# A gated linear attention feeding a cosine-gated MLP: scores as 48x128 products, value sums and state products in 64-channel pieces, independence by parts

## The chip, the cores and the metric

The kernel runs on one core of a Trainium2 chip. The metric is the device time in microseconds (us) of one execution; lower is better. TensorE (PE) does matrix products into PSUM, VectorE (DVE) and ScalarE (ACT) work on PSUM and SBUF, GpSimd (POOL) on SBUF alone, and SyncE (SP) issues most DMAs. A TensorE product has two instructions: a load of the stationary operand (PEld in the profile) and a matmul that streams the moving operand through it. The array can be divided: a product with a stationary operand of at most 64 rows or columns can be given a part of it, and products on different parts can run at the same time. A "tile size" below is that division: 128x128 is the whole array, 64x64 a quarter, 128x32 a column strip.

## The reference, cut to what matters

```python
def _attn_ref(q, k, v, f_logit):            # (B, H, S, D) = (4, 8, 768, 48)
    f = 1.0 / (1.0 + np.exp(-f_logit))
    state = np.zeros((B, H, D, D))
    for t in range(S):
        state = f[:, :, t, :, None] * state + np.einsum('bhd,bhe->bhde', k[:, :, t], v[:, :, t])
        y[:, :, t] = np.einsum('bhd,bhde->bhe', q[:, :, t], state)
    return y

def _moe_ref(x, w_in, w_out):               # x: (3072, 384), d_ff = 2048
    h = x @ w_in
    g = h * np.cos(h)
    return g @ w_out
```

The attention output, 8 heads of 48 channels side by side (384 channels), is x of the second part. All inputs and the output are float32.

## The kernel before, in words

The recurrence is computed in chunks of 128 tokens, two chunks (g = 0, 1) at a time. Such a pair, n = 0 to 11, is 256 tokens of one batch; three pairs make a batch. Within a pair: gates and their running sums (ex, ln, cum, eb, ei), q and k scaled by them (qm, km), q and k turned so that channels lie on partitions, scores, masked scores, value sums, state products, and the state update. The names below are the steps of the code; `n` is the pair, and a second number the half of the heads (u) or the chunk.

- **tq/tk, qkt.** Pairs 0 to 6 are turned on TensorE (`tr`, L436, against an identity, 8 transposes for a half of the heads) and copied out of PSUM by DVE or ACT. Pairs 7 to 11 (`TURN_QK`) are turned by a DMA transpose on SP's queue instead; these the code calls `turned`.
- **sc, am.** `scores` (L456) multiplies k by q for four heads, 16 products of 48 rows by 64 columns, whose places in the array are r (rows 0 or 64) and x (columns 0 or 64). DVE masks them on the way to SBUF (am, L460).
- **ps, st, sz.** `outer` (L478) forms k times v; DVE adds the old state (st, L496) and scales by the decay (sz, L502).
- **y, yi.** `inner` (y) multiplies values by masked scores, `inter` (yi) the old state by q, both into the same PSUM sum of 384 channels by 256 tokens. Both go through `summed` (L530), which cuts the 384 channels into 12 blocks of 32 columns and orders the products so that four neighbours lie on four different column strips. A head of 48 channels touches two blocks, and its zero-padded values (tile vt) fill the rest.
- **xe.** DVE or ACT copies each chunk's sum to x (L199, the line of a shared copy helper).

The second part runs over units of 128 or 256 tokens (unit m of 2 to 12 is pair m - 1): h (L578) is x times w_in, co (L583) the cosine on ACT, g (L560) the product on DVE, o (L594) g times w_out, ot the copy and out the store. Step h11.21 is unit 11, quarter 2, half 1.

The order of all steps on all engines, with the engine and the PSUM bank or SBUF slot of each, is a list written out by a planner and fixed in the string `ORDER`. Its letters are T for PE, S for ACT, V for DVE, G for POOL, Y for SP. It interleaves the attention of later pairs with the products of earlier units. PSUM is four tiles of two banks each. Two steps on different engines that touch the same PSUM tile would be made to wait for each other; `apart` (L644) declares such a pair independent when their banks differ and they share no SBUF slot.

Step `zf` is a product of zeros that fills TensorE's idle time in the first part of the kernel.

Of the kernel before, what the change touches and what calls it, by code (L numbers as in the profile page):

```python
# [10 lines left out]
BF16 = mybir.dt.bfloat16  # L11
# [4 lines left out]
B, H, S, D = 4, 8, 768, 48  # L16
C = 128
PAIRS = B * S // (2 * C)
PPB = S // (2 * C)
DM, DF = 384, 2048  # L20
# [170 lines left out]
def describe(nc, cpool, ppool, q, k, v, f_logit, moe_w_in, moe_w_out, out):  # L191
# [3 lines left out]
    def tl(shape, dt, name):  # L195
        return cpool.tile(shape, dt, name=name)

    def copy(e, o, i):
        (nc.scalar.copy if e == "ACT" else eng(e).tensor_copy)(out=o, in_=i)  # L199
# [6 lines left out]
    ident = tl([128, 128], BF16, "ident")  # L206
# [4 lines left out]
    if nc is not None:  # L211
# [5 lines left out]
        for r in range(2):  # L217
            s = slice(64 * r, 64 * r + 64)
# [94 lines left out]
    def pair(n):  # L313
        b, c = divmod(n, PPB)
# [49 lines left out]
        if not cut:  # L364
            G.step(f"ad{n}", ("POOL",), lambda e: eng(e).tensor_add(  # L365
                out=sp.ap[:, 0, :, 0:D], in0=soft.ap[:, :, 0, :], in1=soft.ap[:, :, 1, :]), reads=[soft], writes=[sp])
# [23 lines left out]
        for nm, dst, dh, sc, w in (("eb", bt, bth, -1.0, HB + 4), ("ei", bi, bih, 1.0, HB)):  # L390
            if cut:
                for u in us:
                    G.step(f"{nm}{n}.{u}", ("ACT",), lambda e, u=u, dh=dh, sc=sc, w=w: nc.scalar.activation(
                        out=dh[u].ap, in_=pcs[u].ap[:, 0:w], func=AF.Exp, scale=sc),
                        reads=[pcs[u]], writes=[dh[u]], table="E")
            else:
                G.step(f"{nm}{n}", ("ACT",), lambda e, dst=dst, sc=sc, w=w: nc.scalar.activation(
                    out=dst.ap, in_=pcs[0].ap[:, 0:2 * (HB + 4)].rearrange("p (u n) -> p u n", u=2)[:, :, 0:w],
# [5 lines left out]
        for u in us:  # L404
            for j, (nm, src, dec) in enumerate((("qm", qh[u], bth[u]), ("km", kh[u], bih[u]))):
                G.step(f"{nm}{n}.{u}", ("POOL", "DVE") if cut else ("POOL",), lambda e, u=u, j=j, src=src, dec=dec: eng(e).tensor_mul(  # L406
                    out=qkp[u][j].ap[:, :, :, 0:D], in0=swap(src.ap),
                    in1=dec.ap[:, 0:HB].rearrange("p (h d) -> p h d", d=D)[:, None].broadcast_to([128, 2, 4, D])),
                    reads=[src, dec], writes=[qkp[u][j]])
        vb, vt = Val(vbS), Val(vtS)  # L410
# [8 lines left out]

        qkt = [Val(qktS), Val(qktS)]  # L420
        turned = n in TURN_QK
        qkv = lambda u: qkt[u].ap.rearrange("p (j e a g n) -> p j a g e n", j=2, a=2, g=2, e=2)
        for u in us:
            if turned:
                G.step(f"tq{n}.{u}", ("SP",), lambda e, u=u: nc.sync.dma_start_transpose(
                    out=qkt[u].ap.rearrange("p (b n) -> p b n", n=C),
                    in_=qk.ap[:, u].rearrange("p j e h d -> p (j e h d)")),
                    reads=[qkp[u][0], qkp[u][1]], writes=[qkt[u]])
                continue
            pt = Val(p1)  # L430

            def tr(e, u, j, pt):
                o = pt.ap.bitcast(BF16).rearrange("p (j e a n) -> p j e a n", j=2, e=2, a=2)
                for x in range(2):
                    for a in range(2):
                        nc.tensor.transpose(out=o[:, j, x, a, :], identity=ident,  # L436
                                            in_=qkp[u][j].ap[:, x, 2 * a:2 * a + 2, :].rearrange("p h d -> p (h d)"))
            for j in range(2):
                G.step(f"t{'qk'[j]}{n}.{u}", ("PE",), lambda e, u=u, j=j, pt=pt: tr(e, u, j, pt),
                       reads=[qkp[u][j]], writes=[pt], sums=True)  # L440
            G.step(f"qkt{n}.{u}", ("DVE", "ACT"), lambda e, u=u, pt=pt: copy(e, qkt[u].ap, pt.ap.bitcast(BF16)),
                   reads=[pt], writes=[qkt[u]])


        am = [Val(amS), Val(amS)]
        for u in us:
            sc = Val(p2)

            def scores(e, u=u, sc=sc):
                o = sc.ap.rearrange("p (r b n) -> p r b n", r=2, n=C)  # L450
                for a in range(2):
                    for g in range(2):
                        for r in range(2):
                            for x in range(2):
                                s, t = slice(64 * r, 64 * r + D), slice(64 * x, 64 * x + 64)
                                nc.tensor.matmul(o[t, r, 2 * a + g, :].rearrange("p (e n) -> p e n", e=2),  # L456
                                                 lhsT=qkv(u)[s, 1, a, g, x, :], rhs=qkv(u)[s, 0, a, g, :, :],
                                                 start=(a == 0 and g == 0), stop=(a == 1 and g == 1))
            G.step(f"sc{n}.{u}", ("PE",), scores, reads=[qkt[u]], writes=[sc])
            G.step(f"am{n}.{u}", ("DVE",), lambda e, u=u, sc=sc: nc.vector.tensor_mul(  # L460
                out=am[u].ap.rearrange("p r b n -> p (r b) n"), in0=sc.ap.rearrange("p (y m) -> p y m", m=C),
                in1=pmask.rearrange("p a n -> p (a n)")[:, None, :].broadcast_to([128, 8, C])),
                reads=[sc], writes=[am[u]])
# [3 lines left out]
        ps = [Val(p1), Val(p1)]  # L467
# [17 lines left out]
        before = [state.get(b), None]  # L485
        for g in gs:
            view = lambda g=g: ps[g].ap[:, 0:HB].rearrange("p (a n) -> p a n", n=D)
            new, S0 = Val(szS), before[g]
# [24 lines left out]
        py = [Val(p1), Val(p1)]  # L513


        def blocks(h):
            i, j = divmod(h, 2)
            return ((3 * i, 16), (3 * i + 1, 48)) if j == 0 else ((3 * i + 1, 0), (3 * i + 2, 32))

        def summed(work, ops):  # L520
            lanes, left = [[w for w in work if w[1] % 4 == c] for c in range(4)], {}
            for w in work:
                left[w[0], w[1] % 4] = left.get((w[0], w[1] % 4), 0) + 1
            begun = set()
            for k in range(max(map(len, lanes))):
                for w in (lane[k] for lane in lanes if k < len(lane)):
                    g, b = w[0], w[1]
                    c, m = b % 4, b // 4
                    left[g, c] -= 1
                    nc.tensor.matmul(py[g].ap[32 * c:32 * c + 32, C * m:C * m + C],  # L530
                                     start=(py[g].first and (g, c) not in begun),
                                     stop=(py[g].final and left[g, c] == 0), **ops(*w))
                    begun.add((g, c))

        def inner(e):
            summed([(g, b, h, at) for g in range(2) for h in range(H) for b, at in blocks(h)],
                   lambda g, b, h, at: dict(lhsT=vt.ap[:, H * g + h, at:at + 32],
                                            rhs=am[h // 4].ap[:, h % 2, h % 4 // 2 * 2 + g, :]))

        def inter(e):  # L540
            summed([(g, b) for g in range(2) if before[g] is not None for b in range(DM // 32)],
                   lambda g, b: dict(
                       lhsT=before[g].ap[:, b // 3].rearrange("p r d -> p (r d)")[:, b % 3 * 32:b % 3 * 32 + 32],
                       rhs=qkv(b // 6)[:, 0, b // 3 % 2, g, :, :]))
        G.step(f"y{n}", ("PE",), inner, reads=[am[0], am[1], vt], writes=py, sums=True)
        G.step(f"yi{n}", ("PE",), inter, reads=[*qkt, *(s for s in before if s is not None)],
               writes=py if before[0] is not None else [py[1]], sums=True)


        x = Val(xS)  # L550
# [56 lines left out]
    for n in range(PAIRS):  # L607
        pair(n)
    t0 = 0
# [9 lines left out]
def emit(tc, G, tiles):  # L619
    nc = tc.nc  # L620
    plan = []
    for word in ORDER.split():
        name, how = word.split(":")
        plan.append((G.steps[name], LETTER[how[0]], [int(x) for x in how[1:].split(",") if x]))
    assert len(plan) == len(G.steps)
    table, users = None, [[] for _ in tiles]
    for s, e, places in plan:
        for w in s.writes:
            v = w.whole
            if v.pool is not None and v.slot is None:  # L630
                v.slot = places.pop(0)
            w.first, w.final = not w.begun, w.left == 1
            w.begun, w.left = True, w.left - 1
        if s.table is not None:
            if s.table == "E" and table != "E":
                nc.scalar.preload_act_table_set("natural_log_exp_and_others")
            table = s.table
        n0 = nc.next_id()
        s.fn(e)
        made = (nc.find_inst_by_name(f"I-{i}") for i in range(n0 + 1, nc.next_id()))  # L640
        apart(tc, users, s, e, [i for i in made if i is not None])


def apart(tc, users, s, e, made):  # L644


    vals = [v.whole for v in s.reads + s.writes]
    banks = {b for v in vals if isinstance(v.pool, Banks) for b in range(v.slot, v.slot + v.pool.size)}
    places = {(v.pool.name, v.slot) for v in vals if v.pool is not None and not isinstance(v.pool, Banks)}
    for t in {b // 2 for b in banks}:  # L650
        for engine, others, theirs, there in users[t]:
            if engine != e and not banks & theirs and not places & there:
                for b in others:
                    for a in made:
                        tc.declare_no_dep(a, b, reason="the steps use different PSUM banks")
        users[t].append((e, made, banks, places))
        del users[t][:-WITHIN]


# [48 lines left out]
```

## Time and profile before

| | us |
|---|---|
| median of 3 runs (lowest to highest) | 189.03 (188.83 to 189.44) |
| the profiled execution | 188.89 |
| its span, first to last instruction | 186.9 |
| PE busy, 2580 matmuls recorded | 177.5 |
| DVE, ACT, POOL busy | 140.1, 136.2, 102.8 |
| L578 and L594 (h and o), busy | 66.4 and 67.4 |
| L530 (y and yi), L456 (sc), busy over the span | 11.12 and 8.81 |

Busy times are unions of the instructions' spans, so overlapping matmuls count once. The span is what the trace covers; some 2.0 us of the execution lie around it. TensorE's granted clock is 1.00 in the whole span.

### The profile page before, as it was taken

Reading aid. Unit: us, or ns where it says so; the run is one execution under the profiler, and the core shown is the slowest. Engines: PE = TensorE matmul, PEld = TensorE weight load, DVE = VectorE, ACT = ScalarE, POOL = GpSimd, SP = SyncE. Lnnn points to the kernel's source line nnn. Section 1 sums busy time; section 2 is a strip of 40 time slices with the busy share of each in tenths; the row PEclk is TensorE's granted clock in tenths of the full one; section 3 lists DMA queues with packets and bytes.
Section 4 is the critical chain, followed back from the end, with each engine's and each line's share of the span. In section 5 each row is a group of like instructions: output and inputs, shape, how many; then the busy total and the mean of one; then the engine's idle time right before and its main releaser. Section 6 shows DMA issues by size and latency. Waiting matters only on the chain.

```text
span 186.9 us, 6052 instructions
## 1 busy us (share of the span) xinstructions
PE 177.5 (95%) x2580; PEld 127.8 (68%) x2584; DVE 140.1 (75%) x209; ACT 136.2 (73%) x196; POOL 102.8 (55%) x131
## 2 busy tenths in 40 slices
PE   7999779999999999999999899999999999999992
PEld 2455437986668976688866787667777888755661
DVE  4458986994897998999997889978999798530010
ACT  3898596795998999798899797897746887500051
POOL 3058249995586998999947999399910000000000
PEclk9999999999999999999999999999999999999999
DMA  6999999639999981996699599977860000000054
GB/s 152 261 261 298 335 355 339 202 102 301 279 265 281 281 189 48 266 282 173 142 259 237 130 230 194 192 194 65 153 186 4 0 4 0 0 0 4 0 212 166
DMA packets 68058, 32.89 MB, mean 176 GB/s; under 512 B 61120, under 2 KB 66496, under 8 KB 68032
## 3 DMA queue, kind: packets, MB, share of 16 engines
q1 hardware_dynamic: 62512, 30.35, 67.5%
q10 hardware_dynamic: 5520, 2.16, 4.9%
q8 instruction: 20, 0.33, 0.8%
q14 instruction: 6, 0.05, 0.1%
HBM read 25.17 MB, written 4.72 MB: 160 GB/s over the span
## 4 chain that ended last, share of the span: by engine, by line
PE 74%; DMA 10%; DVE 6%; POOL 4%; ACT 3%; issue 1%; ACTq 0%; POOLq 0%; DVEq 0%
PE ps L578 32%; PE ps L594 32%; DMA k<-in_k_dram 8%; PE ps L456 3%; PE ps L530 3%; DMA f<-in_f_logit_dram 2%; PE ps L436 2%; DVE sz L502 2%; DVE ps L496 2%; POOL qk L406 2%; PE ps L478 1%; DVE am L460 1%; DVE x L199 1%; POOL k L353 1%; ACT sp L335 1%
## 5 line engine op out<-in xcount | busy, mean ns | idle before, releaser
L594 PE MATMUL ps<-w_out_bf,g 128*128 128x384 bf16 x384 | 67.4, 326 | 0.0
L578 PE MATMUL ps<-x,w_in_bf 128*128 128x256 bf16 (+1 forms) x624 | 66.4, 264 | 1.0 <-DVE sz L502 0.5
L560 DVE TENSOR_TENSOR g<-ps,co 128x1024 bf16<-128x1024 f32 x48 | 61.2, 1312 | 7.0 <-ACT co L583 6.7
L583 ACT ACTIVATE co<-ps,halfpi 128x1024 bf16<-128x1024 f32 x48 | 52.6, 1114 | 14.0 <-PE ps L578 11.5
L578 PEld LDWEIGHTS <-w_in_bf 128*128 128x128 bf16 x624 | 56.6, 98 | 8.8 <-DVE sz L502 1.0
L594 PEld LDWEIGHTS <-g 128*128 128x128 bf16 x384 | 35.9, 98 | 22.0
L460 DVE TENSOR_TENSOR am<-ps,pmask 128x1024 bf16<-128x1024 f32 x24 | 28.7, 1219 | 4.6 <-PE ps L456 4.2
L406 POOL TENSOR_TENSOR qk<-k,bi 128x384 bf16<-128x384 f32 x22 | 21.8, 1004 | 0.6
L199 ACT COPY ot<-ps 128x384 f32<-128x384 f32 (+1 forms) x16 | 6.9, 461 | 20.0 <-DVE ot L199 15.4
L353 POOL TENSOR_TENSOR k<-k,f 128x384 f32<-128x384 f32 (+1 forms) x12 | 11.2, 936 | 16.4 <-DMA k<-in_k_dram 9.4
L406 POOL TENSOR_TENSOR qk<-q,b 128x384 bf16<-128x384 f32 x20 | 19.8, 1004 | 0.6
L199 DVE COPY ot<-ps 128x384 f32<-128x384 f32 (+1 forms) x10 | 5.0, 511 | 18.2 <-PE ps L594 15.3
L266 PE MATMUL ps<-zero 128*128 128x512 bf16 x58 | 17.0, 427 | 1.5 <-DVE zero L205 1.2
L199 POOL COPY vt<-vb 64x384 bf16<-64x384 bf16 x29 | 14.6, 503 | 2.2 <-ACT vb L199 0.8
L502 DVE TENSOR_TENSOR sz<-ps,b 64x192 bf16<-64x192 f32 x40 | 13.9, 354 | 1.3 <-PE ps L478 0.3
L365 POOL TENSOR_TENSOR sp<-ls 128x384 bf16<-128x384 f32 x10 | 10.0, 1000 | 8.0 <-ACT ls L335 7.9
L496 DVE TENSOR_TENSOR ps<-ps,sz 64x192 f32<-64x192 f32 x32 | 11.7, 366 | 2.3 <-PE ps L530 0.9
L436 PE MATMUL ps<-ident,qk 128*128 128x128 bf16 x112 | 9.9, 219 | 2.4 <-POOL qk L406 1.3
L331 ACT ACTIVATE f<-f 128x768 f32<-128x768 f32 (+1 forms) x14 | 10.4, 749 | 1.9 <-DMA f<-in_f_logit_dram 1.7
L199 DVE COPY qkt<-ps 128x1024 bf16<-128x1024 bf16 x12 | 8.1, 683 | 4.5 <-PE ps L436 4.4
L436 PEld LDWEIGHTS <-qk 128*128 128x128 bf16 x112 | 7.5, 98 | 5.2 <-DVE qk L406 1.6
L266 PEld LDWEIGHTS <-zero 128*128 128x128 bf16 x62 | 5.7, 105 | 7.3 <-issue 2.2
(62 smaller groups left out, 176.3 us busy)
## 6 DMA issues: line engine op xcount, KB each, us to landing
v<-in_v_dram SPq DMA_DIRECT2D x12, 384.0 KB, 6.7
out_dram<-ot SPq DMA_DIRECT2D x22, 192.0 KB, 2.2
f<-in_f_logit_dram SPq DMA_DIRECT2D x9, 384.0 KB, 4.3
q<-in_q_dram SPq DMA_DIRECT2D x9, 384.0 KB, 5.9
k<-in_k_dram SPq DMA_DIRECT2D x9, 384.0 KB, 5.4
g<-in_moe_w_in_dram SPq DMA_DIRECT2D x4, 768.0 KB, 10.7
g<-in_moe_w_out_dram SPq DMA_DIRECT2D x4, 768.0 KB, 7.6
q<-in_q_dram SPq DMA_DIRECT2D x3, 192.0 KB, 5.3
```

Of the source, the lines that this page charges most:

```text
L199: (nc.scalar.copy if e == "ACT" else eng(e).tensor_copy)(out=o, in_=i)
L266: G.step(f"zf{i}", ("PE",), lambda e, dump=dump: nc.tensor.matmul(dump.ap, lhsT=zero[:, 0:128], rhs=zero, start=True, stop=True), writes=[ ...
L353: eng(e).tensor_mul(out=w.ap[:, :, 0, :], in0=w.ap[:, :, 0, :], in1=t.ap[:, :, 0, :])
L406: G.step(f"{nm}{n}.{u}", ("POOL", "DVE") if cut else ("POOL",), lambda e, u=u, j=j, src=src, dec=dec: eng(e).tensor_mul(out=qkp[u][j].ap[: ...
L436: nc.tensor.transpose(out=o[:, j, x, a, :], identity=ident, in_=qkp[u][j].ap[:, x, 2 * a:2 * a + 2, :].rearrange("p h d -> p (h d)"))
L460: G.step(f"am{n}.{u}", ("DVE",), lambda e, u=u, sc=sc: nc.vector.tensor_mul(out=am[u].ap.rearrange("p r b n -> p (r b) n"), in0=sc.ap.rear ...
L496: nc.vector.tensor_add(out=view()[s], in0=view()[s], in1=S0.ap[s, :, r, :])
L502: eng(e).tensor_mul(out=new.ap[s, :, r, :].rearrange("p (u a) n -> p u a n", u=2), in0=view()[s].rearrange("p (u a) n -> p u a n", u=2), i ...
L560: nc.vector.tensor_mul(out=o.rearrange("p b (n e) -> p b e n", e=2), in0=ph.ap.rearrange("p (b e n) -> p b e n", e=2, n=64), in1=co.ap.rea ...
L578: nc.tensor.matmul(ph.ap[:, i * T:(i + 1) * T].rearrange("p (g t) -> p g t", t=C), lhsT=w_in_bf[:, kk, f0:f0 + 128], rhs=xa[:, :, kk, :], ...
L583: G.step(f"co{m}.{j}", ("ACT",), lambda e, ph=ph, co=co: nc.scalar.activation(out=co.ap, in_=ph.ap, func=AF.Sin, bias=halfpi), reads=[ph], ...
L594: nc.tensor.matmul(po.ap[:, 0:DM], lhsT=gT.ap[:, j, i * C:(i + 1) * C], rhs=w_out_bf[:, j, :], start=(po.first and j == 4 * s), stop=(po.f ...
```

## The change

Three edits. `ORDER` stays as it is.

1. **Scores.** For the pairs that TensorE turns (0 to 6), the layout of the turned q and k becomes `(j a g e n)`: the two token halves e of a chunk lie side by side, so that a head's k of a chunk is 128 contiguous columns. `scores` then makes 8 products of 48 rows by 128 columns for four heads instead of 16 of 48 by 64. The transposes write their 128 columns in two strides of 64. Pairs 7 to 11 keep the layout and the 16 products.
2. **Pieces.** `pieces` cuts a range of channels into pieces of 64 where one starts on a multiple of 64 and fits, and of 32 elsewhere. Heads 0, 3, 4 and 7 become one piece of 64 each, heads 1, 2, 5 and 6 two of 32. In `inter`, each two heads (96 channels) become one of 64 and one of 32. Both steps issue the wide pieces first.
3. **Independence.** `apart` compared slots by name. Now two steps meet in an SBUF slot only where one of them writes it and they use the same part of the value, or one uses the whole, or the slot holds different values.

```diff
-        qkv = lambda u: qkt[u].ap.rearrange("p (j e a g n) -> p j a g e n", j=2, a=2, g=2, e=2)
+        order = "p (j e a g n) -> p j a g e n" if turned else "p (j a g e n) -> p j a g e n"
+        qkv = lambda u: qkt[u].ap.rearrange(order, j=2, a=2, g=2, e=2)
...
-                o = pt.ap.bitcast(BF16).rearrange("p (j e a n) -> p j e a n", j=2, e=2, a=2)
+                o = pt.ap.bitcast(BF16).rearrange(order, j=2, a=2, g=2, e=2)
...
-                        nc.tensor.transpose(out=o[:, j, x, a, :], identity=ident,
+                        nc.tensor.transpose(out=o[:, j, a, :, x, :], identity=ident,
...
+                cuts = ((0, 64), (64, 128)) if turned else ((0, 128),)
...
-                            for x in range(2):
-                                s, t = slice(64 * r, 64 * r + D), slice(64 * x, 64 * x + 64)
-                                nc.tensor.matmul(o[t, r, 2 * a + g, :].rearrange("p (e n) -> p e n", e=2),
-                                                 lhsT=qkv(u)[s, 1, a, g, x, :], rhs=qkv(u)[s, 0, a, g, :, :],
+                            for t0, t1 in cuts:
+                                s, wide = slice(64 * r, 64 * r + D), qkv(u)[:, 1, a, g]
+                                nc.tensor.matmul(o[t0:t1, r, 2 * a + g, :].rearrange("p (e n) -> p e n", e=2),
+                                                 lhsT=wide[s, t0 // 64, :] if turned else wide[s].rearrange("p e n -> p (e n)"),
+                                                 rhs=qkv(u)[s, 0, a, g, :, :],
...
-        def blocks(h):
-            i, j = divmod(h, 2)
-            return ((3 * i, 16), (3 * i + 1, 48)) if j == 0 else ((3 * i + 1, 0), (3 * i + 2, 32))
+        def pieces(c0, c1):
+
+            while c0 < c1:
+                w = 64 if c0 % 64 == 0 and c1 - c0 >= 64 else 32
+                yield c0, w
+                c0 += w
...
+                nc.tensor.matmul(py[g].ap[at:at + width, c0 // 128 * C:c0 // 128 * C + C],
+                                 start=(py[g].first and new[0]),
+                                 stop=(py[g].final and all(left[t] == 0 for t in lanes(w))), **ops(*w))
...
         def inner(e):
-            summed([(g, b, h, at) for g in range(2) for h in range(H) for b, at in blocks(h)],
-                   lambda g, b, h, at: dict(lhsT=vt.ap[:, H * g + h, at:at + 32],
-                                            rhs=am[h // 4].ap[:, h % 2, h % 4 // 2 * 2 + g, :]))
+            work = []
+            for hs in ((0, 4), (3, 7), (1, 5), (2, 6)):
+                for g in range(2):
+                    both = [list(pieces(D * h // 32 * 32, -(-(D * h + D) // 32) * 32)) for h in hs]
+                    work += [(g, *p, h, 16 + p[0] - D * h) for ps in zip(*both) for p, h in zip(ps, hs)]
+            summed(work, lambda g, c0, w, h, at: dict(lhsT=vt.ap[:, H * g + h, at:at + w],
+                                                      rhs=am[h // 4].ap[:, h % 2, h % 4 // 2 * 2 + g, :]))
 
         def inter(e):
...
+            work = [(g, c0, w, i, c0 - 2 * D * i) for g in range(2) if before[g] is not None
+                    for i in (0, 2, 1, 3) for c0, w in pieces(2 * D * i, 2 * D * i + 2 * D)]
+            work.sort(key=lambda w: -w[2])
...
-    places = {(v.pool.name, v.slot) for v in vals if v.pool is not None and not isinstance(v.pool, Banks)}
+    home = lambda v: v.whole.pool is not None and not isinstance(v.whole.pool, Banks)
+    uses = [(v, v.whole, i) for i, vs in enumerate((s.reads, s.writes)) for v in vs if home(v)]
+
+    def meet(theirs):
+        for v, w, wr in uses:
+            for v2, w2, wr2 in theirs:
+                if (wr or wr2) and w.pool is w2.pool and w.slot == w2.slot:
+                    if w is not w2 or v is v2 or v is w or v2 is w2:
+                        return True
+        return False
...
-            if engine != e and not banks & theirs and not places & there:
+            if engine != e and not banks & theirs and not meet(there):
```

More of the change, by code (lines that the diff above doesn't have):

```diff
@@ L513, in pair @@
         py = [Val(p1), Val(p1)]
-        def blocks(h):
-            i, j = divmod(h, 2)
-            return ((3 * i, 16), (3 * i + 1, 48)) if j == 0 else ((3 * i + 1, 0), (3 * i + 2, 32))
+        def pieces(c0, c1):
[3 more added lines that the diff above has]
+                c0 += w
         def summed(work, ops):
-            lanes, left = [[w for w in work if w[1] % 4 == c] for c in range(4)], {}
+            left, begun = {}, set()
+            lanes = lambda w: [(w[0], (w[1] % 128 + i) // 32) for i in range(0, w[2], 32)]
@@ L522, in summed @@
             for w in work:
[L523 to L533, printed above, removed]
@@ L535, in inner @@
-        def inner(e):
-            summed([(g, b, h, at) for g in range(2) for h in range(H) for b, at in blocks(h)],
-                   lambda g, b, h, at: dict(lhsT=vt.ap[:, H * g + h, at:at + 32],
-                                            rhs=am[h // 4].ap[:, h % 2, h % 4 // 2 * 2 + g, :]))
-        def inter(e):
[L541 to L544, printed above, removed]
+                for t in lanes(w):
+                    left[t] = left.get(t, 0) + 1
@@ new lines, in summed @@
+            for w in work:
+                g, c0, width = w[:3]
+                at = c0 % 128
+                new = [t not in begun for t in lanes(w)]
+                assert all(new) or not any(new)
+                for t in lanes(w):
+                    left[t] -= 1
+                nc.tensor.matmul(py[g].ap[at:at + width, c0 // 128 * C:c0 // 128 * C + C],
+                                 start=(py[g].first and new[0]),
+                                 stop=(py[g].final and all(left[t] == 0 for t in lanes(w))), **ops(*w))
+                begun.update(lanes(w))
@@ L545, in pair @@
+        def inter(e):
+            work = [(g, c0, w, i, c0 - 2 * D * i) for g in range(2) if before[g] is not None
+                    for i in (0, 2, 1, 3) for c0, w in pieces(2 * D * i, 2 * D * i + 2 * D)]
+            work.sort(key=lambda w: -w[2])
+            summed(work, lambda g, c0, w, i, at: dict(
+                       lhsT=before[g].ap[:, i].rearrange("p r d -> p (r d)")[:, at:at + w],
+                       rhs=qkv(i // 2)[:, 0, i % 2, g, :, :]))
         G.step(f"y{n}", ("PE",), inner, reads=[am[0], am[1], vt], writes=py, sums=True)
@@ L655, in apart @@
                         tc.declare_no_dep(a, b, reason="the steps use different PSUM banks")
-        users[t].append((e, made, banks, places))
+        users[t].append((e, made, banks, uses))
         del users[t][:-WITHIN]
```

## The prediction

> **What bounds the kernel now.** I read the page first: engine totals, then the chain of work that ended last.
>
> ```profile
> PE 177.5 (95%) x2580; PEld 127.8 (68%) x2584; DVE 140.1 (75%) x209; ACT 136.2 (73%) x196; POOL 102.8 (55%) x131
> PEclk9999999999999999999999999999999999999999
> PE 74%; DMA 10%; DVE 6%; POOL 4%; ACT 3%; issue 1%; ACTq 0%; POOLq 0%; DVEq 0%
> ```
>
> TensorE is busy 95% of the span at full clock and carries 74% of the chain. The chain's DMA pieces all lie before 25.9 us; from 31.8 us on it runs on PE with short excursions to DVE and ACT, and from 144.1 to 183.4 us it is PE alone. So a step added on PE costs its full time unless PE was idle next to it, and an idle stretch is worth what it is long. Next I need the price of the edited matmuls, from the timeline of PE around a scores step (L456), and then around yi5 and y5 (both L530).
>
> ```profile
> 140.00 0.27 PE L578 MATMUL ps<-x,w_in_bf 128*128 128x256 bf16 x1
> 140.20 0.42 PE L456 MATMUL ps<-qkt 48*64 48x128 bf16 x16
> 140.56 0.39 PE L578 MATMUL ps<-x,w_in_bf 128*128 128x256 bf16 x2
> ```
>
> ```profile
> 83.65 0.27 PE L578 MATMUL ps<-x,w_in_bf 128*128 128x256 bf16 x1
> 83.85 0.52 PE L530 MATMUL ps<-qkt,sz 128*32 128x128 bf16 x24
> 84.20 0.62 PE L530 MATMUL ps<-am,vt 128*32 128x128 bf16 x32
> 84.75 0.34 PE L594 MATMUL ps<-w_out_bf,g 128*128 128x384 bf16 x1
> ```
>
> The first column is the start. Between the two L530 rows nothing changes shape: 24 matmuls in 84.20 - 83.85 = 0.35 us. They run four at a time (four column groups of 32), so six rounds of 0.058. Full-array matmuls of the same 128 moving columns, the transposes of L436 in the chain, take as long each:
>
> ```profile
> 44.12 0.22 PE ps L436 x4
> ```
>
> 0.22 / 4 = 0.055, each with new weights. A round therefore costs its 128 columns, whether one, two or four matmuls share it. The other price is the edge. An L578 matmul is followed by the next after 0.109 (84 in 9.35 us on the chain, waits included; 12 in 1.31 without), but the L530 block starts 83.85 - 83.65 = 0.20 after one: 0.09 lost. From 83.65 to 84.75 are 1.10 us, of which 0.109 is the L578 matmul and 14 x 0.056 = 0.78 are rounds: 0.21 for two changes of the array's division, 0.105 each. Around the scores: 0.56 - 0.109 - 4 x 0.056 = 0.23, or 0.115 each.
>
> Last, the idle places, from PE's, ACT's and DVE's timelines.
>
> ```profile
> 57.29 0.38 PE L578 MATMUL ps<-x,w_in_bf 128*128 128x256 bf16 x2 [0.29 <-ACT x L199]
> 105.40 0.28 PE L578 MATMUL ps<-x,w_in_bf 128*128 128x256 bf16 x1 [0.49 <-DVE sz L502]
> ```
>
> ```profile
> 56.76 0.48 ACT L199 CAST x<-ps 128x384 bf16<-128x384 f32 x1 [0.86 <-DVE x L199]
> 143.59 0.48 ACT L199 CAST x<-ps 128x384 bf16<-128x384 f32 x1 [1.76 <-DVE x L199]
> ```
>
> ```profile
> 103.21 0.77 DVE L496 TENSOR_TENSOR ps<-ps,sz 64x192 f32<-64x192 f32 x2 [0.90 <-PE ps L530]
> ```
>
> xe2.1 and xe10.0 on ACT wait for the other half's copy on DVE, and st7.10 on DVE waits for yi7, though they share no data: the old, coarse independence.
>
> **The change, part by part.** Matmuls fall from 2584 to 2296: scores 7 pairs x 16 = 112, `inner` 12 x 8 = 96, `inter` 20 x 4 = 80. *The rounds do not fall.* Scores: 16 matmuls four abreast (64x64) or 8 two abreast (64 rows x 128 columns), four rounds both. `inner`: 32 / 4 = 8 rounds before; now 8 / 2 + 16 / 4 = 8. `inter`: 24 / 4 = 6; now 8 / 2 + 8 / 4 = 6. Saved array time: none. I cost the strided transposes and contiguous score operands at nothing: same elements, and 0.055 is already the streaming rate. Should they cost, waits for inputs cover it until 31.8 us; after that a tenth more on some 70 transposes is 0.4 us.
>
> *What is added is edges.* Each `inner` and `inter` now begins with 64-wide pieces and ends with 32-wide ones, and adjacent steps change back. Counting tile sizes in the built PE stream: 57 changes before, 98 after. Of the 41 new ones 38 lie between 128x64 and 128x32, 3 between 64x64 and 64x128. No row has a change between two column widths; all seen are to or from 128x128, or between 64x64 and 128x32, and those all lose 0.09 at once and 0.105 with the slower first round. I take 0.105, bounded by 0.093 and 0.117; below, nothing excludes zero, which is a rival.
>
> *What the declaration by parts removes* (waits in the built program): xe2.1 on xe2.0, xe5.1 on xe5.0, xe10.0 on xe10.1, st7.10 on yi7. In exchange h3.20, h5.10 and h11.21 on PE now wait for both copies of their x, with all of PE queued behind, and xe7.0 on DVE for yi7; the walk shows each done in time. A few loads wait on another DMA semaphore (v7, q6, out6, tq7.0), each of a transfer whose data is used earlier; nothing, unless one is late, and then it holds the SP or ACT queue by that lateness. The order on every engine is as before, so nothing is moved past a queue.
>
> Now the walk, D being PE's delay, idle read off the rows:
> - To 32 us, 5 new changes (yi0, y0, yi1/y1): 0.5 us in waits for inputs; the last, tq3.1 for qm3.1 on POOL, has 0.43 idle for the 0.315 of yi1/y1. D = 0.
> - 55.1 to 57.3, y2 yi2 yi3 y3: 7 changes, 0.735. Idle: yi3 at 56.19, 0.33 after yi2's rounds, since sz3.01 ends at 56.13; h3.20 0.36 after y3, for xe2.1. With xe2.1 freed and DVE free at 56.13, both copies are through by 57.0, before PE. D = +0.05.
> - 70 to 74.5, ps4.1 to sc4.0: +0.105; cum6 idles 0.25 for DVE and POOL, whose chain from ps4.1 is unmoved. D = 0.
> - 75.7 to 77.4, yi4 y4 (3) and ps5.1 to sc5.1 (1): 0.42 against sc5.0's idle of 0.34 for qkt5.0 on DVE, busy without a break since 70.6. D = +0.08.
> - 83.8 to 88.2, yi5 y5: 0.315 against 0.14 before h6.21, waiting for DVE. D = 0.255.
> - About 95, sc7.0 (64x64) to sc6.0 (64x128): D = 0.36.
> - 101.7 to 105.4, y6 y7 yi7 yi6: 0.735 against 0.22 before y7 (sz7.00) and 0.66 before h7.00 (12 x 0.109 after 103.43 is 104.74). That 0.66 was DVE's st7, xe7.0, sz7 run started late by yi7; now the two L496 adds (0.77) run during y7, and DVE is through by 105.2, PE at about 105.6. D = 0.215.
> - 127.3, y8 yi8: 0.315 less 0.07 before ps10.0. D = 0.46.
> - 134.2, yi9 y9: D = 0.775.
> - 142 to 144.1, y10 yi10 y11 yi11: 0.735 less 0.21 before y11 and 0.22 before h11.21, both copies of xe10 being through 0.5 before PE. D = 1.08.
> After 144.1 us PE runs alone, so D lasts. 36 changes x 0.105 = 3.78 went in, 2.7 of idle took it up. The profiled execution took 188.89 (span 186.9 and 2.0 around it), 0.14 below the median of 189.03. The sum gives 189.97 for it, 190.1 for a median; I say 190.0. At 0.093 a change the same walk gives D = 0.7, at 0.117 1.4: 189.6 to 190.5.
>
> **Rivals.** *Changes between column widths are free* (the other side). The three changes left cost 0.3, and freed waits show: 0.36 at h3.20, 0.66 at h7.00, 0.22 at h11.21. The second and third are PE-side gains in full; the first may be swallowed by the DVE waits at 74 to 77. Sum -0.8 to -1.1: 188.1. For it: no row shows this change. Against: the loss is the same 0.09 whether columns alone change (128x128 to 128x32) or rows too. It decides below 0.06 a change, where the walk crosses zero; at 0.05 to 0.08 it ends within 0.3%. The Trainium skill, "TensorEngine Tiling (Array Packing)", section "Key Properties", says that changing the tiling mode, not only the tile, drains TensorE. By that rule all 41 changes cost; the rows agree for the six pairs of shapes they hold and are silent on this one.
>
> *Scores with 128 columns on 64 rows wait for weights.* A 64-column load hides in a 0.056 round; were 128 columns on half the rows twice as slow, four rounds would cost 0.22 more per scores step, ten of them after 32 us, sc4 partly covered: +2.1, 192.1. Against: L436 loads 128 columns at 0.055 each, though on the whole array. The Trainium skill, "TensorE: Matmul & The Clock Gate", section "Weight-path perf modes", has the fast weight load on when the number of weights is 128 and the type is not FP32; that favours no loss, and no run here shows it.
>
> *Matmuls cost by the piece.* Busy time per instruction, from the sums of the two lines over stretches:
>
> ```profile
> sum 186.90, PE 11.12 PEld 8.97; mean PE 1.85 PEld 1.50
> sum 186.90, PE 8.81 PEld 6.24; mean PE 1.47 PEld 1.04
> ```
>
> 11.12 / 624 = 0.0178 for L530, 8.81 / 384 = 0.0229 for L456. After 32 us 148 and 80 go: 4.5 us less, 184.6. The fixed round of four speaks against it. That would also be the change doing what its count suggests.
>
> **Chances.** Forecast 0.62; width changes at half price or so, near no change, 0.10; free 0.13; slow score weights 0.12; by the piece 0.03. About 0.3% (0.57 us) is what a measurement of this kernel can tell from no change: above 189.60 lie nine tenths of the forecast and the slow weights, 0.68; below 188.46 the free case and the count, 0.16; between, 0.16. The range runs from the free case, 187.9, to the forecast's upper bound with a margin for scores a little slower, 190.8; outside are 0.15. The forecast's own range is 189.6 to 190.5.
>
> **What would show it.** Right: inside L530's block a start 0.15 (a round and 0.09) after the last wide piece; rounds still 0.056, two matmuls in each wide one; h3.20 and h7.00 no longer idle for x and sz; ACT's xe10.0 beside DVE's xe10.1; PE through its last L594 about 1 us later. Wrong: wide rounds near 0.1, scores steps over 0.4 between neighbours' starts, or width changes at 0.056.

## The result, and the profile after

The changed kernel takes 190.37 us (median of 5 runs, 190.25 to 190.77) against 189.12 (188.83 to 189.53) for the kernel before on the same chip: 1.0066 times as long, 95% interval 1.0047 to 1.0085. The forecast was 190.0. In single executions of some kernels TensorE's clock ran at half for a stretch; the medians, ratios and ranges below leave those out, and where a profile holds such a stretch the text says so.

The page of the changed kernel, engine totals and the chain by engine:

```profile
PE 180.5 (96%) x2292; PEld 128.1 (68%) x2296; DVE 140.0 (74%) x209; ACT 136.6 (72%) x196; POOL 102.9 (55%) x131
PE 83%; DMA 10%; ACT 2%; POOL 2%; issue 0%; ACTq 0%; DVE 0%; POOLq 0%; DVEq 0%
```

288 fewer matmuls, yet TensorE is busy 3 us longer, and DVE's 6% of the chain has gone to it. The busy time of L540 (y and yi, L530 before) over the span says where: 15.04 us with 448 matmuls, where L530 had 11.12 with 624.

```profile
sum 188.70, PE 15.04 PEld 9.78; mean PE 2.51 PEld 1.63
```

The timeline of PE around yi5 and y5, then around y10 to yi11. A row shows the shape of its first pieces, the 64-wide ones; the 32-wide follow in the same row.

```profile
84.39 0.64 PE L540 MATMUL ps<-qkt,sz 128*64 128x128 bf16 x16
84.96 0.75 PE L540 MATMUL ps<-am,vt 128*64 128x128 bf16 x24
85.65 0.34 PE L610 MATMUL ps<-w_out_bf,g 128*128 128x384 bf16 x1
```

```profile
143.29 0.27 PE L594 MATMUL ps<-x,w_in_bf 128*128 128x256 bf16 x1
143.49 0.75 PE L540 MATMUL ps<-am,vt 128*64 128x128 bf16 x24
144.17 0.64 PE L540 MATMUL ps<-qkt,sz 128*64 128x128 bf16 x16
144.74 0.75 PE L540 MATMUL ps<-am,vt 128*64 128x128 bf16 x24
145.42 0.64 PE L540 MATMUL ps<-qkt,sz 128*64 128x128 bf16 x16
145.99 0.28 PE L594 MATMUL ps<-x,w_in_bf 128*128 128x256 bf16 x1
```

yi5 and y5 took 0.90 us from the first start to the next step's; now it is 85.65 - 84.39 = 1.26. In the second block PE never waits: 2.70 us from the L594 matmul to the next, of which 0.109 is that matmul and 28 x 0.056 = 1.57 are rounds. (A round is a set of matmuls that share the array side by side.) The other 1.02 are nine changes of the array's division, 0.114 each. Start by start inside the rows, the first narrow round begins 0.149 after the last wide one: a round of 0.056 and 0.093 lost. The change back costs the same 0.093. The round right after a change is slower, 0.080 when wide and 0.067 when narrow; the others are 0.056 in both widths, two matmuls in a wide round and four in a narrow one.

The freed waits, on ACT for xe2.1 and on DVE for st7.10, then the starts of h3.20 (57.71) and of h6.31 with h7.00 behind it (105.01) on PE:

```profile
56.75 0.48 ACT L199 CAST x<-ps 128x384 bf16<-128x384 f32 x1 [0.57 <-PE ps L540]
```

```profile
103.20 0.77 DVE L499 TENSOR_TENSOR ps<-ps,sz 64x192 f32<-64x192 f32 x2
```

```profile
57.71 0.50 PE L594 MATMUL ps<-x,w_in_bf 128*128 128x256 bf16 x3
105.01 1.70 PE L594 MATMUL ps<-x,w_in_bf 128*128 128x256 bf16 x14
```

xe2.1 starts when the sum is ready and beside xe2.0; DVE's two adds start at 103.20, as early as before, though PE finishes yi7 more than a us later. Neither h3.20 nor h7.00 waits any more: the row from 105.01 runs through the 12 matmuls of h6.31 into h7.00. ACT's xe10.0 and DVE's xe10.1 both start at 144.86.

### The profile page after: what moved, and what is told of

It reads as the page before. It is cut to its first block, busy times and chain, and to the rows that moved or that the text cites. A ratio compares the mean times of both kernels' runs of the same rounds, so it can differ in the third digit from the quotient of the medians.

```text
span 188.7 us, 5479 instructions
## 1 busy us (share of the span) xinstructions
PE 180.5 (96%) x2292; PEld 128.1 (68%) x2296; DVE 140.0 (74%) x209; ACT 136.6 (72%) x196; POOL 102.9 (55%) x131
## 4 chain that ended last, share of the span: by engine, by line
PE 83%; DMA 10%; ACT 2%; POOL 2%; issue 0%; ACTq 0%; DVE 0%; POOLq 0%; DVEq 0%
PE ps L610 34%; PE ps L594 33%; DMA k<-in_k_dram 8%; PE ps L540 7%; PE ps L458 3%; PE ps L437 3%; DMA f<-in_f_logit_dram 3%; PE ps L481 2%; PE ps L376 1%; POOL k L353 1%; ACT sp L335 1%; ACT f L331 1%; POOL qk L406 1%; PE ps L382 0%; POOL vt L199 0%
## 5 line engine op out<-in xcount | busy, mean ns | idle before, releaser
L594 PE MATMUL ps<-x,w_in_bf 128*128 128x256 bf16 (+1 forms) x624 | 66.1, 264 | 0.0
L594 PEld LDWEIGHTS <-w_in_bf 128*128 128x128 bf16 x624 | 56.6, 98 | 7.3 <-issue 0.3
L343 POOL TENSOR_TENSOR q<-f,q 128x384 f32<-128x384 f32 x10 | 10.0, 1001 | 2.5 <-DMA q<-in_q_dram 1.5
```

The lines of the kernel that those rows point to most:

```text
L594: nc.tensor.matmul(ph.ap[:, i * T:(i + 1) * T].rearrange("p (g t) -> p g t", t=C), lhsT=w_in_bf[:, kk, f0:f0 + 128], rhs=xa[:, :, kk, :], ...
```

## The experiments

Five kernels separate the parts of the change; six more follow up a surprise in the fifth or check the rest. Each was timed beside the kernel before, whose median there stands in brackets.

### Independence by parts alone

`apart` of the changed kernel in the kernel before; nothing else.

```diff
...
-            if engine != e and not banks & theirs and not places & there:
+            if engine != e and not banks & theirs and not meet(there):
...
```

> The kernel before with the independence by parts alone: no wide piece, 57 changes of tile size as before. Theory A (each change of the array's division costs TensorE about 0.11 us, and the freed waits lie beside the path): the idle before h3.20 (0.36), h7.00 (0.66) and h11.21 (0.22) goes, so 0.8 to 1.1 us less than the kernel before: 188.2. Rival B (the freed waits only move the idle to the next wait): 189.0. Rival C (the new waits of h3.20, h5.10 and h11.21 for both copies hold PE, and that is what the change costs): 189.5 or more.

Measured: 187.70 (189.01), ratio 0.9934 (0.9902 to 0.9966). Faster than both kernels, and 1.3 below the kernel before, where 0.8 to 1.1 was expected. Rivals B and C fall. PE's and DVE's timelines:

```profile
101.88 0.93 PE L530 MATMUL ps<-am,vt 128*32 128x128 bf16 x38
102.62 0.69 PE L530 MATMUL ps<-qkt,sz 128*32 128x128 bf16 x36
103.24 1.70 PE L578 MATMUL ps<-x,w_in_bf 128*128 128x256 bf16 x14
```

```profile
102.16 0.77 DVE L496 TENSOR_TENSOR ps<-ps,sz 64x192 f32<-64x192 f32 x2
103.03 0.56 DVE L199 CAST x<-ps 128x384 bf16<-128x384 f32 x1
```

The adds run at 102.16, inside y7, not after yi7, and L578 goes through h6.3 into h7.00 (14 matmuls in the row) without the pause. Counted from 33 us, PE gains 0.34 at h3.20, 0.66 at h7.00 and 0.21 at h11.21, 1.2 in all: the three idle stretches that the prediction listed, in full.

### The changed kernel with the old independence

```diff
...
-            if engine != e and not banks & theirs and not meet(there):
+            if engine != e and not banks & theirs and not places & there:
...
```

> The changed kernel with the old, coarse independence: 98 changes of tile size as in the changed kernel. Theory A: the copies of x2 and x10 follow one another again and st7 waits for yi7 again; the idle before h3.20 and h7.00 stays and the new edges come on top, about 0.3 and 0.4 more than the changed kernel: 191.0. Rival B (the freed waits are worth nothing): 190.4, as the changed kernel. Rival C: below the changed kernel, 189.9.

Measured: 191.16 (189.01), ratio 1.0102 (1.0066 to 1.0138), 0.8 above the changed kernel, as theory A has it; rivals B and C fall. Its DVE timeline shows the wait back, with the new edges in it:

```profile
105.19 0.77 DVE L499 TENSOR_TENSOR ps<-ps,sz 64x192 f32<-64x192 f32 x2 [1.40 <-PE ps L540]
```

In this trace, of an execution of 191.83, PE loses only 0.15 at h3.20 and 0.14 at h7.00 themselves. Ahead of them lie 0.34 more before y2, mostly a wait for POOL, and 0.26 more in a stall without a wait (last section), and both use up part of these idle places. So the sum fits the forecast, but its split is not shown by this run.

### Fewer changes of width

The second of y and yi into a sum begins with the width that the step before ended with.

```diff
         def summed(work, ops):
+            lead = 64 if any(py[w[0]].first for w in work) else at_width[0]
+            work = sorted(work, key=lambda w: w[2] != lead)
+            at_width[0] = work[-1][2]
...
-            work.sort(key=lambda w: -w[2])
```

> The changed kernel, where the second of y and yi into the same sum begins with the width that the step before ended with: the same 2296 matmuls, 87 changes of tile size instead of 98, 10 of the 11 fewer after 32 us. Theory A: the walk with 0.104 per change to 32 and 0.117 per change to 64 gives 0.8 less than the changed kernel: 189.6. Rival F (the wide pieces themselves are slow, not the changes between widths): no difference to the changed kernel, 190.4.

Measured: 189.61 (189.01), 0.76 below the changed kernel with the same products in the same pieces. Between the two traces PE gains 0.95 after 32 us. Rival F falls.

### More changes of width

```diff
-            for hs in ((0, 4), (3, 7), (1, 5), (2, 6)):
+            for hs in ((0, 4), (1, 5), (3, 7), (2, 6)):
```

> The changed kernel with the heads of y in the order (0, 4), (1, 5), (3, 7), (2, 6) instead of (0, 4), (3, 7), (1, 5), (2, 6): the same products in the same pieces, but each y goes wide, narrow, wide, narrow; 122 changes of tile size instead of 98, 20 of the 24 more after 32 us. Theory A (each change costs TensorE 0.104 to 32 columns, 0.117 to 64, and the idle is used up): 2.2 more than the changed kernel, 192.6. Rival F (wide pieces themselves slow): no difference, 190.4.

Measured: 192.79 (189.12), ratio 1.0193 (1.017 to 1.0215): 2.42 above the changed kernel for 20 changes after 32 us, 0.12 each. Its PE timeline at y10, to be held against the second block above, and then that of the kernel before:

```profile
145.07 0.99 PE L540 MATMUL ps<-am,vt 128*64 128x128 bf16 x24
145.99 0.64 PE L540 MATMUL ps<-qkt,sz 128*64 128x128 bf16 x16
```

```profile
141.98 0.63 PE L530 MATMUL ps<-am,vt 128*32 128x128 bf16 x32
142.44 0.51 PE L530 MATMUL ps<-qkt,sz 128*32 128x128 bf16 x24
```

One y, from its start to yi's: 142.44 - 141.98 = 0.46 in the kernel before (no change on the way), 144.17 - 143.49 = 0.68 in the changed one (two), 145.99 - 145.07 = 0.92 here (four). The time goes with the changes: 0.11 to 0.12 each, whatever the number of matmuls (32, 24, 24).

### Parts and 48x128 scores, y and yi in 32s

The changed kernel with `blocks`, `summed`, `inner` and `inter` of the kernel before.

> The kernel before with the independence by parts and the 48x128 scores, y and yi in pieces of 32 as before: 2472 matmuls, 60 changes of tile size. Theory A: three changes between 64x64 and 64x128, two of them beside idle time, so 0.1 above the kernel with parts alone: 188.3. Rival D (the products with 128 columns on 64 rows wait for their weights): 1 us or more above it. Rival E (matmuls cost by the piece): 80 fewer after 32 us at 0.023 are 1.8 below it.

Measured: 189.35 (189.01), with a spread from 188.58 to 190.51. That is 1.65 above parts alone, where 0.1 was expected: by the times, rival D. But the profile does not show it in the scores. PE's timeline at y3:

```profile
57.09 0.35 PE L533 MATMUL ps<-am,vt 128*32 128x128 bf16 x12
59.07 0.46 PE L533 MATMUL ps<-am,vt 128*32 128x128 bf16 x20 [1.63 <-issue]
```

TensorE stops 12 matmuls into a step of 32, at its 735th weight load, with no wait. Packets of 16 KB come in on the instruction queue all through the span, 19 here; one ran from 56.3 to 57.6 us. TensorE goes through y2, yi2, yi3 and y3, some 200 instructions, in under 2 us. So a third theory, G: the stall is the arrival of instructions, and where it falls depends on what precedes it in TensorE's stream. (This execution, of 190.51, spans 2.8 us more than that of parts alone: 1.8 at this stall, 0.3 in a wait for POOL before y2, 0.3 in a second stall at the 1503rd load, and the rest in small steps.)

### Moving the stream: three tries with the 48x128 scores, one without

First, 64 small products of zeros in idle time, 128 instructions:

```diff
+                for _ in range({50: 30, 61: 34}.get(i, 0)):
+                    nc.tensor.matmul(dump.ap[:, 0:2], lhsT=zero[:, 0:128], rhs=zero[:, 0:2], start=True, stop=True)
```

> The kernel with parts and 48x128 scores again, with 64 small products of zeros (2 columns each) added in TensorE's idle time at 21 and 26 us: they move what follows by 128 instructions in TensorE's instruction stream and nothing else. In the run without them TensorE stood still for 1.6 us in the middle of y3 with no wait, at a place that is a multiple of 256 instructions in the stream, while an instruction packet of 16 KB was on its way. Theory G (that stall was the arrival of instructions in the densest stretch, and no cost of the scores): no stall in y2 to y3, 188.1, near the kernel with parts alone (187.7), with a smaller spread. Rival D (the 48x128 scores cost it): 189.5 again.

Measured: 189.68 (189.12). No stall in y2 to y3, and from 33 us to the end PE keeps its distance to the kernel with parts alone within 0.13. But the median did not fall. The profile, of an execution of 192.84, is 1.4 us behind parts alone before the first small product and has two more losses. The later one, a late store at the end, comes up again below. The earlier one is in these stretches; PEclk is the last number but two:

```profile
16.00:31.00 15.00, 13.13 (x232) 8.36 (x234) 11.93 (x24) 11.83 (x18) 7.08 (x10) 1.00 1.10 336
31.00:34.40 3.40, 3.40 (x52) 3.01 (x50) 1.94 (x3) 0.33 (x1) 3.18 (x5) 0.50 1.08 361
34.40:56.00 21.60, 21.60 (x274) 16.61 (x267) 17.43 (x17) 18.00 (x20) 15.71 (x15) 1.00 0.75 187
```

The granted clock fell to half for 3.4 us. That cannot be what holds the median up: the mean granted clock of this execution is 0.984, that of the others 0.992 to 1.0. Still, the stream was next moved without thinning the early work, by cutting zero products of 512 columns into four of 128, and the reverse was tried too: the same shift for the kernel with parts alone, which had no stall.

```diff
-                dump.ap, lhsT=zero[:, 0:128], rhs=zero, start=True, stop=True), writes=[dump])
+                w = 512 // (4 if 36 <= i < 57 else 2 if i == 57 else 1)
+                for c0 in range(0, 512, w):
+                    nc.tensor.matmul(dump.ap[:, c0:c0 + w], lhsT=zero[:, 0:128], rhs=zero[:, 0:w], start=True, stop=True)
```

> The kernel with parts alone (187.7), with 21 of the zero products between 18 and 25 us cut into four of 128 columns and one into two: the same zero columns, 128 more instructions in TensorE's stream ahead of y2, so that y3 lies against the 256-instruction blocks as it did in the kernel with parts and 48x128 scores, where TensorE stood for 1.6 us in it. Theory G (the stall is the arrival of instructions in the dense stretch y2 to y3): a stall of up to 1.6 us in y3 in some or all executions, 188.5 to 189.3, wider spread. Rival D (the stall had to do with the 48x128 scores): 187.8, no stall.

Measured: 189.47 (188.93), 189.22 to 190.24: 1.8 above parts alone. No wide score, no wide piece, and the stall is there, again 12 matmuls into y3, now at the 863rd weight load, 128 loads (256 instructions) after the 735th:

```profile
56.82 0.35 PE L533 MATMUL ps<-am,vt 128*32 128x128 bf16 x12
59.28 0.46 PE L533 MATMUL ps<-am,vt 128*32 128x128 bf16 x20 [2.11 <-issue]
```

A packet had come in from 56.8 to 57.8. In this execution, of 192.11, the clock then dropped to half from 60.0 to 63.4, and 1.7 us more were lost there:

```profile
60.00:63.40 3.40, 3.40 (x18) 2.42 (x17) 2.34 (x8) 1.11 (x1) 3.32 (x5) 0.51 0.80 189
```

Without these 1.7 it would have taken some 190.4; that the stall is in the others too is read from their times alone. Rival D falls as the cause of the stall.

> The kernel with parts and 48x128 scores, with the zero products cut in the same way: y2 to y3 now lie against the blocks as in the kernel with parts alone. TensorE's activity in the early part is not thinned, as it was by the small products of the earlier attempt, in whose profile the granted clock fell to half from 31.0 to 34.4 us. Theory G: no stall, 0.1 to 0.4 above the kernel with parts alone, 187.9 to 188.1, narrow spread. Rival D: 189.5.

Measured: 189.78 (188.93), 189.47 to 189.98. Not the number expected. The profile has no stall, and PE starts its last products 0.15 earlier than with parts alone (0.17 earlier at 33 us), so the scores took 0.02. The 2 us were lost behind PE, in the chain's last pieces:

```profile
177.82 4.16 DMA out_dram<-ot
182.02 0.17 ACT ot L199
182.19 1.99 DMA out_dram<-ot
```

The last instruction packet ran from 177.9 to 179.7, beside that store. The same is in the trace with small products: the store was issued at 181.2 and the last instruction packet ran from 181.4 to 182.9.

> Parts and 48x128 scores once more, with 32 zero products before 25 us cut into four each: 192 more instructions ahead of y2 instead of 128. In the run with 128 the scores cost nothing that could be seen (TensorE reached the last products 0.15 before the kernel with parts alone did), but a store issued at 177.8, together with the last 16 KB instruction packet at 177.9, took 4.2 us instead of about 2 and the end came 2 us later. Theory G (the last instruction packet delayed that store): the same block is now reached 64 instructions, some 5 us, earlier, before the last stores, and the end is not late: 187.8, as the kernel with parts alone. Rival D (the scores cost it): 189.5.

Measured: 189.69 (188.94), 188.86 to 191.10; again not the number. The end was not late in the profile (188.96), but the same block boundary, the 863rd load, now fell before h4.11, and PE stood 1.08 us there:

```profile
59.50 0.71 PE L584 MATMUL ps<-x,w_in_bf 128*128 128x256 bf16 x5 [0.90 <-DVE vt L233]
```

The row names DVE's clearing of vt, but with parts alone the same matmul started at 58.45, before that DVE step began (58.90), so it is not what the matmul needs. Without the stall the span of 186.9 would be 185.8, beside 185.7 for parts alone. No try got rid of every stall and late store, so that the scores cost nothing is read from three traces, not from a median. As to the store: from its issue to its last data packet it took 3.7 and 3.5 us in the two traces in which the last instruction packet lies beside it, and 1.7 us in each of the other eleven, in this run too, where the packet had ended by 174.9. So the two go together; in what way the one delays the other is not shown.

### The changed kernel without its wide scores, and with its stream moved

The transposes, layout and `scores` of the kernel before in the changed kernel (95 changes of tile size), with 28 small products of zeros for alignment:

> The changed kernel with the scores, transposes and layout of the kernel before (64x64), and 28 small products of zeros in idle time at 21 us, so that the instruction stream around y2 to y3 lies as in the kernel before; 95 changes of tile size. Theory A: three changes fewer, and where they lie the idle was eaten in the changed kernel, so 0.2 to 0.3 less than that: 190.1. Rival E (matmuls by the piece): 1.8 more than the changed kernel.

Measured: 190.40 (189.12), 190.05 to 191.23. The medians do not resolve the 0.2 to 0.3; between the two traces PE gains 0.1 at each of sc4, sc5.1 and sc6.0, the three edges, and 0.1 before h6.31, where the changed kernel has a stall. Rival E falls: 1.8 are not there.

The changed kernel with its 32 later zero products cut in four:

> The changed kernel with the same 32 zero products cut into four: the place where its TensorE stood for 0.12 without a wait before h6.31 (a multiple of 256 instructions) now lies elsewhere, the edges stay. Theory A with G: 0.1 less than the changed kernel, 190.3, and no stall before h6.31. Rival (the edges are cheap and instruction arrival is what the change costs): 1 us less, 189.4.

Measured: 190.72 (188.94), 190.56 to 191.51. The stall of 0.12 before h6.31 is gone from the trace, and the rest of PE's timeline stays within 0.07 of the changed kernel's up to there. The time does not fall by 1 us: instruction arrival is not what the change costs. The median is 0.35 above that of the changed kernel instead of 0.1 below; between the two traces (190.72 and 190.77) PE does gain 0.11 at h6.31, and where the medians part is not shown.

## Why the prediction was right

**Mechanism.** A round costs its 128 columns: right, 0.056 with two or four matmuls in it. The loss at a change of column width, of which no row had existed: right, the same 0.093 as at the six kinds seen; the two counts of changes (87 and 122) settle it against F, and the idle of h3.20, h7.00 and h11.21 is freed as listed. The Trainium skill ("TensorEngine Tiling (Array Packing)", section "Key Properties") says that a change of tiling mode drains TensorE; the traces agree for a change of width alone, at 0.093 lost. The weights of 128 columns on 64 rows do not wait: the rounds of the wide scores are 0.056 (first 0.066). The strided transposes cost nothing, as assumed: 9.8 us busy for 112, where they had taken 9.9.

**The sizes, step by step.** PE's delay between the two profiled executions, from the starts of the named steps; the first row is the one the walk had at zero, its five new changes lying beside waits for inputs:

| stretch | forecast | measured | read at |
|---|---|---|---|
| to 32 us | 0 | +0.33 | tq3.1, 31.79 and 32.12 |
| y2 yi2 yi3 y3 | +0.05 | +0.13 | y2 55.09 and 55.38, h3.20 57.29 and 57.71 |
| sc4 | -0.05 | +0.01 | cum6, 74.45 and 74.89 |
| yi4 y4, sc5.1 | +0.08 | +0.10 | h5.00, 81.14 and 81.68 |
| yi5 y5 | +0.175 | +0.22 | h6.21, 88.17 and 88.93 |
| sc6.0 | +0.105 | +0.10 | sc6.1, 94.86 and 95.72 |
| y6 y7 yi7 yi6 | -0.145 | +0.07 | h7.00, 105.40 and 106.33 |
| y8 yi8 | +0.245 | +0.27 | ps10.0, 128.47 and 129.67 |
| yi9 y9 | +0.315 | +0.33 | ps11.1, 134.90 and 136.43 |
| y10 yi10 y11 yi11 | +0.305 | +0.34 | h11.21, 144.12 and 145.99 |

After 32 us the steps add to 1.57 where 1.08 was forecast. The mis-sized term is the price of a change: 0.105, taken from blocks of narrow rounds, is 0.114 with the slower first wide round (36 x 0.009 = 0.32); the bound of 0.117 held it. The widest gap is y6 to yi6, where 0.12 is the stall before h6.31 and 0.06 the price on seven changes. With these two, 0.05 of the 0.49 stays open. Of the first row it is not known how much is the change: at that point the traces of three more kernels with the same five changes (the old independence, and the last two above) stand 0.43, 0.23 and 0.40 behind the kernel before, that of parts alone, without them, 0.14. The median moved by 1.25, not by the 1.88 of these two executions (188.89 and 190.77): the one before was quick for its kernel and the one after slow, the 0.33 of the first row among it. So the forecast of 1.0 is nearer to the median than its own steps were to this pair, and that much of it is luck.

**What was not on the list.** Nothing in the prediction allowed for TensorE's instructions arriving late. In the changed kernel that was worth 0.12; in neighbours of it 0.2 to 2 us.

## What to carry to other kernels

When small matmuls share the array, count rounds and changes of the array's division, not matmuls: merging two into one of twice the width saved nothing, and each place where the width changed cost 0.11 us unless TensorE was idle beside it. A relaxed dependency declaration is worth the idle that the false wait left before the busiest engine. It can be read off the idle column beforehand: 0.36, 0.66 and 0.22 were listed here, 1.3 us were gained by the declaration alone, and that was the whole of what the change had to give (187.70). And an experiment that changes an instruction count moves everything after it in the stream: look for stalls without a wait before blaming the edit.

## What the runs showed of the hardware that was not expected

- **Instructions can arrive late.** TensorE stood 1.1 to 2.1 us without a wait of its own at its 735th or 863rd weight load, 256 instructions apart, whatever the code there was. Smaller stalls, 0.12 to 0.38 us, stand before h6.31: at the 1375th load in the changed kernel, with the old independence and with fewer changes of width, and at the 1503rd with parts and 48x128 scores. All seven places are whole multiples of 128 loads, or 256 instructions, apart; most places on that grid were passed without a stall. At each of the seven, TensorE went on 1.3 to 1.6 us after a 16 KB packet of the instruction queue had come in, and ahead of each lay one of the dense stretches of y and yi. No view shows the arrival itself; it is the reading that fits all of this.
- **A stall can cost twice.** The granted clock went to half for 3.4 us (0.51 in that stretch) 0.7 us after the stall of 2.1 us had ended, and 1.7 us more were lost; a dip of the same length followed early work thinned by tiny products. In the 3.4 us before these dips TensorE was busy for 1.29 us (56.6 to 60.0) and 1.89 us (27.6 to 31.0). Around the stall of 1.6 us the two such stretches (55.0 to 58.4 and 58.4 to 61.8) have 2.12 and 2.73 us, and the clock stayed at 1.00. The Trainium skill, "TensorE: Matmul & The Clock Gate", section "Part 1: The HAM clock gate", has half the clock as the idle state, after an idle window of about 3.4 us. The two dips agree in clock and length, but neither stretch before them was wholly idle.
- **The first round after a change is slower** by 0.024 when 64 columns wide and 0.011 when 32, on top of the 0.093.
